# A cached-attention decode kernel: K in whole softmax blocks, query broadcast by PE, one loop per engine

## Chip, cores, metric

One core of one Trainium2 chip. The metric is the device time of one execution in microseconds (us); lower is better. A change counts as faster or slower when it moves the time by more than 2%.

## The reference

One token attends to 65536 cached keys in each of 16 heads; the result is gated by a small MLP and added to the input. Cut to what matters:

```python
B, Sq, D = 1, 1, 448
H, Sk, Dh = 16, 65536, 256            # k_cache, v_cache: 1 x 16 x 65536 x 256, bfloat16
xn = _layernorm(x)
q = (xn @ wq).reshape(B, Sq, H, Dh).transpose(0, 2, 1, 3)
scores = jnp.einsum("bhqd,bhkd->bhqk", q, k_cache) * (Dh ** -0.5)
p = _softmax(scores, axis=-1)
o = jnp.einsum("bhqk,bhkd->bhqd", p, v_cache)
s = o.transpose(0, 2, 1, 3).reshape(B, Sq, H * Dh) @ wo
g = silu(silu(xn @ w1) @ w2)
return x + s * g
```

K and V are 1074 MB together, the weights some 10 MB. Each cached number is used once.

## The kernel before

The cache is cut into 64 blocks of 128 x 128 keys, four for each head. A partition holds 128 keys of a block, 64 KiB. VectorE (DVE) computes 19 of every 32 dot products with a fused multiply-add and multiplies the other 13 in one instruction; ScalarE (ACT) sums those 13. Then comes a softmax over the block with the block's own maximum, and TensorE (PE) multiplies the weights by V. The blocks' results are combined at the end. SP issues all large loads, in order, into one queue. K and V come in tiles of 64 keys per partition (32 KiB), two tiles of each.

```python
KT = 64; SUB = 32; ND = 19; TPB = 2
Kt = [pool.tile([P, KT * Dh], bf16, name=f"K{t}") for t in range(TPB)]
Vt = [pool.tile([P, KT * Dh], bf16, name=f"V{t}") for t in range(TPB)]
...
def take(e, s, k=1):                       # wait for a semaphore and take k from it
    e.wait_ge(s, k).then_inc(s, -k)

def sp_block(i):
    for t in range(TPB):
        take(sp, kf[t])                    # K's tile is free
        sp.dma_start(out=Kt[t][:, :], in_=src(Kd, i, t)).then_inc(kl[t], 16)
        take(sp, vf[t])                    # V's tile is free
        sp.dma_start(out=Vt[t][:, :], in_=src(Vd, i - 1, t)).then_inc(vl[t], 16)

def dve_block(i, first=False, halves=False):
    q_t = own(dve.tensor_copy(out=qcur[:, :], in_=qb[:, sub(q0, Dh)]))
    for t in range(TPB):
        for s in range(2):                 # four steps of 32 keys
            k = t * 2 + s
            if s == 0:
                take(dve, kl[t], 16)       # half a block has landed
            ...
            m = dve.tensor_tensor(out=prod[k % 2][:, :, :], ...)       # 13 keys, for ACT
            if (k == 0 and not first) or (k == 2 and halves):
                dve_gmax()                 # global maximum of the block before
            for j in range(ND):            # 19 keys, fused
                ins = dve.tensor_tensor_reduce(out=junk_d[jk][:, :], ...,
                    accum_out=S[:, k * SUB + j : k * SUB + j + 1])
    ...
    end(0, TPB * KT, kf[1])                # copy S, row maximum for PE

with nc.Fori(1, NBLK - 1, 1, engines={ET.PE, ET.DVE, ET.Activation, ET.SP}, ...) as i:
    sp_block(i)
    dve_block(i)
    act_block(i)
    act_keep(i - 1)
    pe_bcast()                             # global maximum to all partitions
    pe_attend()                            # weights times V
    pe_rows()                              # row maxima to one row
    pe_turn()                              # turn the block's result
...
# after the loop: the last V has a place of its own, W, where the query's weights lay
take(sp, vf[0])
halves(Vt[0], src(Vd, last, 0), vh[0:2])
halves(W, src(Vd, last, 1), vh[2:4])
...
pe_bcast()
pe_attend(between=half_max)                # V's first tile, then half_max
half_max()                                 # pe_rows(), pe_bcast()
```

## Time and profile before

| | before |
|---|---|
| time, median of 4 runs | 2528.03 us (2527.88 to 2528.26) |
| span of the profiled execution | 2527.2 us (that execution took 2529.32 us, 1.3 above the median) |
| mean granted TensorE clock | 0.727 |
| DVE busy | 2219.2 us, 88% |
| DMA, rate from 300 to 2300 us, from the packet records | 431.7 GB/s |

The page, the windows and DVE's steps are shown in the prediction below. Timeline columns: start, duration, engine, line, operation, output<-inputs, count, and in brackets the idle time before it with what ended it.

```profile
2470.90 9.02 PE L308 MATMUL psO<-V,PV 128*2 128x512 bf16 x32 [7.32 <-PEq L141]
...
2486.54 9.73 PE L308 MATMUL psO<-V,PV 128*2 128x512 bf16 x32 [5.24 <-PEq L141]
...
2498.88 8.69 PE L308 MATMUL psO<-V,PV 128*2 128x512 bf16 x32
...
2518.48 4.70 PE L679 MATMUL ps_ao<-K,OT 128*1 128x448 bf16 x24
```

A block's V is 64 matmuls, half of it 32. The last block but one is multiplied at 2470.90 and 2486.54, as its two tiles come. From 2486.54 PE hardly waits again, and ends at 2518.48 + 4.70 = 2523.2. The last byte of data lands about 2517.3.

### The profile page before, as it was taken

To read this page: it belongs to the slowest core of one execution; us is meant where nothing else is said; L and a number is where in the kernel's file an instruction comes from. 1 tells how busy PE (TensorE), PEld (TensorE's weight loads), DVE (VectorE), ACT (ScalarE), POOL (GpSimd) and SP (SyncE) were. 2 spreads that over 40 slices of the span, in tenths; PEclk is the share of its full clock that TensorE was granted. 3 is DMA by queue.
4 is the path that set the end of the run, shared out by engine and by line. 5 is a ranking of instruction groups with operands and counts; after the bars stand their busy time and mean duration, and the time that the engine had idled before them with its cause. 6 is when DMAs were issued, how large, how long until landed. Compare 5 with 4: busy or idle time off the path is not lost. (4 is left out here: it accounts for less than half of the span.)

```text
span 2527.2 us, 30558 instructions
## 1 busy us (share of the span) xinstructions
PE 1284.5 (51%) x4945; PEld 483.4 (19%) x4945; DVE 2219.2 (88%) x10276; ACT 1446.6 (57%) x6996; POOL 1.4 (0%) x12
## 2 busy tenths in 40 slices
PE   3554455455544554555455445544554455445547
PEld 1111121111111211111112111111121111111212
DVE  7989898898898988988989889889898898898886
ACT  5656565655565656555656565556565655565553
POOL 0000000000000000000000000000000000000000
PEclk7777777777777777777767776777677767776778
DMA  9999999999999999999999999999999999999998
GB/s 413 432 432 432 432 432 432 432 432 432 432 432 433 432 433 432 432 432 432 432 432 432 432 432 432 432 432 432 432 432 432 432 432 433 432 432 432 432 432 346
DMA packets 40450, 1084.46 MB, mean 429 GB/s; under 512 B 4338, under 2 KB 6516, under 8 KB 6644
## 3 DMA queue, kind: packets, MB, share of 16 engines
q1 hardware_dynamic: 40434, 1084.31, 99.8%
q8 instruction: 4, 0.07, 0.0%
q14 instruction: 10, 0.08, 0.0%
q10 hardware_dynamic: 2, 0.00, 0.0%
HBM read 1084.29 MB, written 0.00 MB: 429 GB/s over the span
## 5 line engine op out<-in xcount | busy, mean ns | idle before, releaser
L262 ACT ACTIVATE junk_a<-prod 128x256 bf16<-128x256 bf16 x3328 | 1330.7, 401 | 746.9 <-ACTq L141 746.9
L308 PE MATMUL psO<-V,PV 128*2 128x512 bf16 x4064 | 1165.2, 458 | 1097.6 <-PEq L141 1097.6
L226 DVE CUSTOM_DVE_ANT_0 junk_d<-K,qcur 128x256 bf16<-128x256 bf16 x4864 | 1698.7, 414 | 0.0
L308 PEld LDWEIGHTS psO<-V,PV 128*2 128x2 bf16 x4064 | 388.4, 97 | 1847.6 <-issue 1520.3
L212 DVE TENSOR_TENSOR prod<-K,qcur 128x3328 bf16<-128x3328 bf16 x256 | 482.9, 1886 | 247.0 <-DVEq L141 247.0
L262 ACT ACTIVATION_READ_ACCUMULATOR junk_a<-prod 128x1 f32 x3328 | 620.0, 186 | 0.0
L226 DVE DVE_READ_ACCUMULATOR2_ANT S<- 128x1 f32 x4864 | 374.2, 77 | 0.0
L295 ACT COPY O<-psO 2x512 f32<-2x512 f32 x64 | 36.8, 574 | 202.4 <-ACTq L141 202.4
L343 PE MATMUL ps_t<-eye,O 2*128 2x1 f32 x520 | 69.6, 251 | 48.4 <-PEq L141 48.4
L343 PEld LDWEIGHTS ps_t<-eye,O 2*128 2x128 f32 x520 | 65.9, 192 | 69.0 <-issue 68.9
L297 ACT COPY hist<-ps_t 128x2 f32 (+1 forms) x65 | 10.4, 160 | 94.9 <-ACTq L141 94.9
L301 PE MATMUL ps_nb<-gmax,ones_row 1*128 1x1 bf16 x65 | 10.3, 159 | 56.1 <-PEq L141 55.6
L191 DVE COPY qcur<-qb 128x256 bf16 (+1 forms) x64 | 14.5, 227 | 25.4 <-issue 15.8
L284 ACT ACTIVATE PV<-S,hist 128x128 bf16<-128x128 f32 (+1 forms) x65 | 26.0, 400 | 2.1
L199 DVE COPY S<-S 128x128 f32<-128x128 f32 (+1 forms) x65 | 14.7, 226 | 9.5
L200 DVE TENSOR_REDUCE rmax<-S 128x1 bf16<-128x128 f32 (+1 forms) x65 | 18.2, 280 | 0.2 <-issue 0.2
L180 DVE TENSOR_REDUCE gmax<-ps_m 1x1 bf16<-1x128 f32 x65 | 17.8, 274 | 0.5 <-DVEq L141 0.5
L301 PEld LDWEIGHTS ps_nb<-gmax,ones_row 1*128 1x128 bf16 x65 | 6.0, 92 | 60.8 <-issue 60.5
L333 PE MATMUL ps_m<-ident,rmax 128*1 128x128 bf16 x65 | 14.3, 220 | 5.7 <-PEq L141 5.7
L488 PE MATMUL ps_a<-xnT,V 128*64 128x1 bf16 x112 | 6.7, 256 | 18.2 <-DMA V<-in_B_w_dram 18.2
L284 ACT ACTIVATION_READ_ACCUMULATOR PV<-S,hist (+1 forms) x65 | 12.1, 186 | 0.0
L488 PEld LDWEIGHTS ps_a<-xnT,V 128*64 128x64 bf16 x112 | 6.6, 210 | 18.7 <-DMA V<-in_B_w_dram 18.7
(65 smaller groups left out, 79.3 us busy)
## 6 DMA issues: line engine op xcount, KB each, us to landing
K<-in_A_k_cache_dram SPq DMA_DIRECT2D x126, 4096.0 KB, 21.3
V<-in_A_v_cache_dram SPq DMA_DIRECT2D x125, 4096.0 KB, 28.7
K<-in_A_k_cache_dram SPq DMA_DIRECT2D x4, 2048.0 KB, 18.5
V<-in_A_v_cache_dram SPq DMA_DIRECT2D x4, 2048.0 KB, 22.9
W<-in_A_v_cache_dram SPq DMA_DIRECT2D x2, 2048.0 KB, 27.3
W<-in_A_wq_dram SPq DMA_DIRECT2D x1, 3072.0 KB, 10.4
K<-in_A_wo_dram SPq DMA_DIRECT2D x3, 896.0 KB, 31.4
V<-in_B_w_dram SPq DMA_DIRECT2D x1, 1568.0 KB, 35.5
```

The lines of the kernel that those rows point to most:

```text
L180: dve.reduce_max(out=gmax[0:1, :], in_=ps_m[0:1, :], axis=AX.X).then_inc(gm, 1)
L191: q_t = own(dve.tensor_copy(out=qcur[:, :], in_=qb[:, sub(q0, Dh)]))
L199: dve.tensor_copy(out=S2[:, c0:c1], in_=S[:, c0:c1]).then_inc(f, 1)
L200: dve.reduce_max(out=rmax[:, :], in_=S[:, c0:c1], axis=AX.X).then_inc(rm, 1)
L212: m = dve.tensor_tensor(out=prod[k % 2][:, :, :], in0=Kv[:, s * SUB + ND : (s + 1) * SUB, :], in1=qcur[:, None, :].to_broadcast([P, NA, Dh ...
L226: ins = dve.tensor_tensor_reduce(out=junk_d[jk][:, :], in0=Kv[:, s * SUB + j, :], in1=qcur[:, :], scale=1.0, scalar=0.0, op0=ALU.mult, op1 ...
L262: ins = act.activation(out=junk_a[jk][:, :], in_=prod[k % 2][:, j, :], func=ACT.Identity, accum_out=S[:, a : a + 1],)
L284: act.activation(out=PV[:, c0:c1], in_=S2[:, c0:c1], func=ACT.Exp, bias=neg, scale=scale, accum_out=hist[:, at(i), 1:2].rearrange("p o s - ...
L295: act.copy(out=O[:, :], in_=po[:, :]).then_inc(oc, 1)
L301: pe.matmul(ps_nb[:, 0:1], lhsT=ones_row[0:1, :], rhs=gmax[0:1, :], start=True, stop=True).then_inc(bm, 1)
L308: ins = pe.matmul(po[:, :], lhsT=PV[:, c0 + c : c0 + c + 2], rhs=T[:, (k0 + c) * Dh : (k0 + c + 2) * Dh], start=(start and c == 0), stop=( ...
L343: ins = pe.matmul(ps_t[:, a : a + 1], lhsT=Ov[:, j, a, :], rhs=eye2[:, j : j + 1], start=(j == 0), stop=(j == 1),)
```

## The change

The intent is fewer and larger transfers and less bookkeeping: K comes as whole blocks in two slots (64 KiB rows, one DMA for each of 63 blocks in place of two; the last still comes in halves), V stays in halves. To find that room, the products overwrite K and the multiplied tile, the query of all heads is no longer kept on every partition (PE broadcasts the head's query once per block), and `W` goes. Each engine gets its own loop; DVE's has two blocks in its body, with a prefetch hint at the branch. DVE now takes its own block's global maximum before it starts the next. The tail is rewritten. The core, with cuts marked by `...`:

```diff
-KT = 64
+KB = 128
+VT = 64
-    Kt = [pool.tile([P, KT * Dh], bf16, name=f"K{t}") for t in range(TPB)]
-    Vt = [pool.tile([P, KT * Dh], bf16, name=f"V{t}") for t in range(TPB)]
-    W = pool.tile([P, max(DF * HD + HD // 2, NHA * D, KT * Dh)], bf16, name="W")
-    prod = [pool.tile([P, NA, Dh], bf16, name=f"prod{i}") for i in range(2)]
-    qb = pool.tile([P, HD], bf16, name="qb")
+    Kt = [pool.tile([P, KW], bf16, name=f"K{t}") for t in range(2)]
+    Vt = [pool.tile([P, VW], bf16, name=f"V{t}") for t in range(2)]
+    prod = pool.tile([P, NA, Dh], bf16, name="prod")
+    q16 = pool.tile([H, Dh], bf16, name="q16")
 ...
+    def load_k(i, s):
+        take(sp, kf[s])
+        sp.dma_start(out=Kt[s][:, :], in_=block(Kd, i)).then_inc(kl[s], 16)
 ...
+        def end(c0, c1, own):
+            ...
+            dve.tensor_copy(out=S2[:, c0:c1], in_=S[:, c0:c1]).then_inc(kf[s], 1)
+            dve.reduce_max(out=rmax[:, :], in_=S[:, c0:c1], axis=AX.X).then_inc(rm, 1)
+            dve_gmax()
+        take(dve, qr)
+        dve.tensor_copy(out=qcur[:, :], in_=ps_q).then_inc(sd, 1)
+        take(dve, kl[s], 16)
+        for k in range(NSTEP):
 ...
                 ins = dve.tensor_tensor_reduce(
-                    out=junk_d[jk][:, :],
+                    out=Kv[:, c, :],
 ...
+    def pe_block(i):
+        take(pe, pv)
+        for t in range(2):
+            take(pe, vl[t], 16)
+            pe_keys(psO, Vt[t], 0, PV, t * VT, VT, t == 0, t == 1, vf[0] if t == 0 else od)
+        pe_rows()
+        pe_turn(vf[1])
+        pe_bcast()
+        pe_query(i + 1)
 ...
+        with loop(ET.SP, 0, NBLK - 4, 2) as i:
+            for s in range(2):
+                load_v(i + s)
+                load_k(i + s + 2, s)
 ...
+        with loop(ET.DVE, 0, NBLK - 2, 2, hint_back_edge=True) as i:
+            for s in range(2):
+                dve_block(s)
 ...
+        project(0)                         # tail: 8 heads' output projection
+        pe_rows()                          # row maxima of half the last block
+        pe_bcast()
+        take(pe, pv)
+        take(pe, vl[0], 16)
+        pe_keys(psO, Vt[0], 0, PV, 0, VT, True, False, vf[0])
+        ...                                # rest of the last block but one
+        act_keep(LAST - 1)
+        pe_turn()
```

## The prediction

The sum: 2528 + 5 - 2 - 1.5 = 2529.5, and 1.5 more for the fetch rival makes the 2531. The quarter for the fetch, the 1% and both ends of the range are estimates. The query matmul's 0.25 us, inside DVE's 2.5, was estimated as half the mean of 458 ns that the page before gives for a 512-column matmul.

> **What bounds the kernel now.** I read the page first (engines, slices), then the table of windows, the SP queue's waits, and the timeline of DVE and PE at a block's edge and in the tail. The page:
>
> ```profile
> span 2527.2 us, 30558 instructions
> PE 1284.5 (51%) x4945; PEld 483.4 (19%) x4945; DVE 2219.2 (88%) x10276; ACT 1446.6 (57%) x6996; POOL 1.4 (0%) x12
> DMA  9999999999999999999999999999999999999998
> GB/s 413 432 432 432 432 432 432 432 432 432 432 432 433 432 433 432 432 432 432 432 432 432 432 432 432 432 432 432 432 432 432 432 432 433 432 432 432 432 432 346
> HBM read 1084.29 MB, written 0.00 MB: 429 GB/s over the span
> ```
>
> DVE at 88% looks like the limit, but DMA is full in every slice but the first and the last, at a constant 432 GB/s, and 1084.29 MB at 432 GB/s is 2510 us of the 2527. The windows say the same, and where the other 17 us are:
>
> ```profile
> 0.00:2.00 2.00, 0.00 (x0) 0.00 (x0) 0.00 (x0) 0.00 (x0) 1.02 (x10) 1.00 0.00 0
> 60.00:2440.00 2380.00, 1205.84 (x4539) 448.55 (x4540) 2115.26 (x9813) 1376.48 (x6684) 0.00 (x0) 0.72 1.00 432
> 2470.00:2504.00 34.00, 25.85 (x95) 9.57 (x96) 30.76 (x134) 18.24 (x88) 0.00 (x0) 0.78 1.01 428
> 2504.00:2517.00 13.00, 13.00 (x66) 5.69 (x65) 2.30 (x8) 1.52 (x4) 0.00 (x0) 1.00 0.95 360
> ```
>
> (Columns: window, length, busy us of PE, weight loads, DVE, ACT, POOL, then clock, DMA share, GB/s.) Two us pass before the first byte; from 60 to 2440 us the DMA share is 1.00; data end near 2517; the rest is PE's tail (its last projection ends at 2523.2), two DVE steps and the output's transfer. A block is 8.39 MB of K and 8.39 MB of V, so the block's period is 16.78 MB / 432 = 38.8 us, 64 times. DVE is busy about 34.5 of them.
>
> DVE's steps, at the end of a block and in the tail, where the row-maximum chain runs with nothing queued before it:
>
> ```profile
> 1206.56 1.89 DVE L212 TENSOR_TENSOR prod<-K,qcur 128x3328 bf16<-128x3328 bf16 x1
> 1208.37 0.42 DVE L226 CUSTOM_DVE_ANT_0 junk_d<-K,qcur 128x256 bf16<-128x256 bf16 x1
> ...
> 1214.59 0.42 DVE L226 CUSTOM_DVE_ANT_0 junk_d<-K,qcur 128x256 bf16<-128x256 bf16 x1
> 1214.93 0.08 DVE L226 DVE_READ_ACCUMULATOR2_ANT S<- 128x1 f32 x1
> 1215.16 0.23 DVE L199 COPY S<-S 128x128 f32<-128x128 f32 x1
> 1215.31 0.28 DVE L200 TENSOR_REDUCE rmax<-S 128x1 bf16<-128x128 f32 x1
> ```
>
> ```profile
> 2496.18 0.21 DVE L200 TENSOR_REDUCE rmax<-S 128x1 bf16<-128x64 f32 x1
> 2496.54 0.22 PE L333 MATMUL ps_m<-ident,rmax 128*1 128x128 bf16 x1 [0.27 <-PEq L141]
> 2496.91 0.28 DVE L180 TENSOR_REDUCE gmax<-ps_m 1x1 bf16<-1x128 f32 x1 [0.51 <-DVEq L141]
> 2497.33 0.16 PE L301 MATMUL ps_nb<-gmax,ones_row 1*128 1x1 bf16 x1 [0.57 <-PEq L141]
> 2497.48 1.07 PE L343 MATMUL ps_t<-eye,O 2*128 2x1 f32 x8
> ```
>
> A step of one multiply and 19 fused multiply-adds is 1214.93 - 1206.56 = 8.37 us. In the second fence each hop between DVE and PE costs about 0.15 us.
>
> [...] the built program's DVE loop has 171 instructions, and between 94 and 2478 us the packet records hold no instruction fetch. The new DVE loop has 339[...].
>
> **The change part by part.**
>
> Bytes: none removed or added. The kernel stays at 2510 us of transfer unless the rate changes.
>
> K in 64 KiB rows. The packet records give a median of 613 ns for 16 KiB and 1218 for 32 KiB: 605 for the second 16 KiB, so about 8 ns are fixed. If a 64 KiB row is one packet, each saves 8 ns: 8 packets per engine and block, 64 blocks, 4.1 us. If it is cut into 32 KiB again, 0. I take 2.
>
> DVE per block, where K is already there: four steps 4 x 8.37 = 33.5 (destination and semaphores change, operand sizes do not). Last fused step to end of row maximum: 1214.93 to 1215.59, 0.66. Then the chain that was hidden in the next block is now on DVE's path, as DVE takes its own global maximum before the next block, and the query comes from PE after PE's turn of the output: hop 0.15, rows 0.22, turn 1.07, global-max broadcast 0.16, query matmul about 0.25 [...], hops 0.3, then the query copy from PSUM, about 0.4 (estimates from the 128-column copy, 0.23). Together about 2.5. DVE's cycle is 33.5 + 0.66 + 2.5 = 36.7 us, longer than before but 2.1 below the DMA's 38.8. ACT's 13 sums take 5.3 us from 0.2 after the multiply, done 1.1 us before the step's end, so one product buffer instead of two costs nothing.
>
> PE per block: two halves of 9.1 to 9.6 us and the small ones, about 21 of 38.8. Not the bound.
>
> Does DMA still always have work? The second half of a block's V waits for PE's turn, which now comes after the end of DVE's next block; so does the K load two blocks on. In steady state DVE's end lies 38.8 - 34.2 = 4.6 us before the next K lands, and half a block of V (9.7 us) is queued behind that K. Some 14 us of work are queued when the issue comes: no gap.
>
> Start: this is where I see a loss. The queue is weights (6.9 MB), K0, K1, V0: K0 lands whole at about 38 us (before, DVE could start on half of it near 21), K1 at 57, V0 at 77. DVE ends block 0 at 38 + 34.5 = 72.5 and block 1 at 72.5 + 36.7 = 109. The queue behind V0 is K2 (to 96) and half of V1 (to 106). The other half of V1 and K3 are released by the end of block 1: first bytes near 111. DMA is idle some 5 us, once. After that DVE gains 2.1 us per block and the margin grows. Against about 0.6 us of loss in before's 40 to 60 us window: +5.
>
> Tail: eight of 16 heads' projection (16 of 32 matmuls of about 0.2 us, 3 us) move ahead of the last V; the last V comes in smaller pieces. In exchange the last DVE block ends 16 us before the last byte instead of 21, still early enough. PE's tail from the last byte: before 2523.2 - 2517 = 6; I get about 5. -1 to -2.
>
> Preamble (64 query matmuls of 16 rows, the diagonal copies): hidden under K0's landing at 38.
>
> Sum: 2528 + 5 (start) - 2 (packets) - 1.5 (tail) = 2529.5. I put 2531 for the rival below.
>
> **The rivals.**
>
> (1) Instruction fetch. [...] But the fetches take time on a DMA engine, and a transfer is done only when its slowest engine is. The trace's 8 KiB instruction packets took 309 ns[...]. [...] I give it a quarter. If the branch also stalls for longer than the two blocks' slack of 4.2 us, DVE becomes the bound: 5 us over it is 31 x 5 = 155, 2680; 5%.
>
> (2) DVE as the bound through the turn-around: each us above 38.8 in its cycle costs 63 us. My 36.7 would have to be 5.7% low. The four steps are measured, so the error must be in the 2.5 us; 4.6 would be needed. Against it: the tail's hops are short. 4%.
>
> (3) The transfer gets faster: [...]
>
> (4) Hidden anyway: everything off DMA's path, 2527 to 2529.
>
> **Range and chances.** Most of the weight lies at 2520 to 2535; the fetch rival stretches the upper side. Centre 2531, range 2517 to 2560. Faster by over 2% would need under 2478[...]: 1%. Slower by over 2% is over 2579: only a bound moved to DVE or a bad fetch: 6%. Within 2%: 93%.
>
> **What would show it.** Right: DMA share 1.00 and 432 to 434 GB/s from 150 us on; a dip in DMA between about 105 and 112 us; DVE busy still near 34.5 of 38.8 us per block, with its idle in two places, some 2 us before the query copy (new) and some 2 before the first multiply (K landing). The packet counts say whether 64 KiB rows are one packet or two. Wrong: a DMA share below 1.00 in the middle, with SP waiting for K's or V's release; DVE with no wait for K; instruction packets in every round; idle DVE at the loop's branch every second block; fused steps slower than 0.346 us apart because they write into K.

## The result and the profile after

| | before | after |
|---|---|---|
| time, median of 4 | 2528.03 us | 2538.82 us (2538.12 to 2539.02) |
| ratio after/before | | 1.0042, 95% interval 1.0025 to 1.0059 |
| span of the profiled execution | 2527.2 us | 2536.9 us |
| clock | 0.727 | 0.713 |

A ratio here is the mean time of one kernel's fast runs over that of the other's fast runs of the same rounds, so not quite the ratio of the medians quoted. The verdict is the same within 2%; the predicted 2531 was 8 us low, inside its range. The profiled executions differ by 9.35 us in time and 9.7 in span; the medians differ by 10.8, because before's profiled execution was 1.3 us above its median. I account for the 9.7.

The page of the kernel after, the lines that answer to those of before:

```profile
span 2536.9 us, 30448 instructions
PE 1217.3 (48%) x5050; PEld 505.8 (20%) x5050; DVE 2234.0 (88%) x10281; ACT 1443.7 (57%) x6991; POOL 2.5 (0%) x13
DMA  9899999999999999999999999999999999999997
GB/s 413 381 432 438 426 433 431 434 433 438 427 433 431 435 441 422 435 432 430 435 441 422 438 430 430 441 427 430 438 430 430 442 426 438 430 430 433 434 419 310
```

The kernel is still bound by DMA; what is lost shows at the edges: 381 in the second slice where before had 432, and 419 and 310 at the end against 432 and 346. The unevenness between (422 to 442) I take for counting, as packets are now up to 64 KiB; the ledger below has an even slope.

**The ledger.** To see where time goes in a kernel bound by transfers, I laid the two packet records over each other: the time at which so many MB had come, from each kernel's first packet, with a packet's bytes spread evenly over its duration. Figures are us; from the third column on, lateness against before.

| MB come | before | after | K in halves | turn last | early start 2 | combined 3 |
|---|---|---|---|---|---|---|
| 40 | 94.3 | +0.2 | 0.0 | 0.0 | -0.4 | -0.4 |
| 50 | 117.4 | +7.8 | +7.6 | +6.6 | +1.1 | +0.2 |
| 100 | 233.2 | +7.4 | +7.6 | +6.2 | +0.8 | 0.0 |
| 400 | 928.1 | +6.0 | +7.5 | +4.8 | -0.6 | -1.4 |
| 1000 | 2317.8 | +3.1 | +7.4 | +1.8 | -3.5 | -4.3 |
| 1060 | 2456.7 | +2.9 | +7.5 | +1.7 | -3.6 | -4.4 |
| 1065 | 2468.4 | +3.9 | +8.3 | +2.6 | 0.0 | -1.9 |
| 1084.2 (end) | 2515.3 | +3.9 | +7.7 | +2.1 | -0.9 | -2.0 |

The column "after" reads: one hole between 40 and 50 MB costs 7.8 us; a slightly higher rate then wins 4.9 of it back over the whole cache; the tail costs 1.0. Data end 3.9 us later than before. The last matmul ends at 2532.9 against 2523.2, 9.7 later, so PE's tail behind the last byte has grown by 9.7 - 3.9 = 5.8 us (from 5.9 to 11.7). 7.8 - 4.9 + 1.0 + 5.8 = 9.7, the span's whole difference. The other columns belong to experiments below.

**The hole.** Before's windows from 104 to 112 us, then after's from 104 to 116 and from the middle (window, length, busy us of PE, weight loads, DVE, ACT, POOL, clock, DMA share, GB/s):

```profile
104.00:108.00 4.00, 4.00 (x16) 1.37 (x14) 3.33 (x20) 2.17 (x12) 0.00 (x0) 0.74 1.05 451
108.00:112.00 4.00, 2.05 (x10) 0.62 (x8) 2.15 (x2) 0.13 (x1) 0.00 (x0) 1.00 0.91 393
```

```profile
104.00:108.00 4.00, 0.00 (x0) 0.00 (x0) 4.00 (x20) 3.10 (x15) 0.00 (x0) 0.50 0.63 270
108.00:112.00 4.00, 0.00 (x0) 0.00 (x0) 3.78 (x22) 2.66 (x13) 0.00 (x0) 0.50 0.02 8
112.00:116.00 4.00, 2.62 (x12) 2.02 (x13) 1.71 (x3) 0.82 (x4) 0.00 (x0) 0.50 0.55 180
...
1000.00:2000.00 1000.00, 479.57 (x1939) 195.40 (x1939) 898.39 (x4148) 582.73 (x2830) 0.00 (x0) 0.71 1.00 433
```

By the shares, after's DMA is empty from about 106.5 to 114. SP has nothing that it may load: the second half of the next V and the next K wait for buffers that come free only with the end of DVE's second block and the turn behind it; SP issues the two at 113.08 and 113.67. In the middle the share is 1.00 again, and stays there.

**DVE's edge of a block.** The timeline of the first one, where nothing waits for DMA:

```profile
74.41 0.28 DVE L223 TENSOR_REDUCE rmax<-S 128x1 bf16<-128x128 f32 x1
...
74.84 0.27 PE L318 MATMUL bank<-ident,rmax 128*1 128x128 bf16 x1 [39.22 <-PEq L153]
...
75.03 1.86 PE L334 MATMUL bank<-eye,O 2*128 2x1 f32 x8
75.25 0.28 DVE L212 TENSOR_REDUCE gmax<-bank 1x1 bf16<-1x128 f32 x1 [0.56 <-DVEq L153]
...
76.76 0.16 PE L324 MATMUL bank<-gmax,ones_row 1*128 1x1 bf16 x1
...
76.79 0.37 PE L348 MATMUL bank<-q,ident 16*128 16x256 bf16 x1
...
77.31 0.43 DVE L227 CAST qcur<-bank 128x256 bf16<-128x256 f32 x1 [1.77 <-DVEq L153]
77.77 1.89 DVE L235 TENSOR_TENSOR prod<-K,qcur 128x3328 bf16<-128x3328 bf16 x1
```

From the end of the row maximum (74.69) to the next multiply (77.77) is 3.08 us, in which DVE works 0.71 and waits 0.56 and 1.77, the two waits in brackets. The longest link is the turn, L334, 1.86 us (eight small matmuls by which PE brings a block's output from two rows back onto the partitions): PE had been idle for 39 us and ran at half clock. In the prediction's row the same eight matmuls took 1.07, behind 9.73 us of matmuls on V. The trace's clock is 0.50 until 82.5 us here, 4.0 us after PE began on V at 78.46, and 1.00 from 2492.0 to 2498.8 around the prediction's row. In the middle of the kernel after it is the same as here: the turn at 1226.16 takes 1.86 us, at a clock of 0.50.

**The tail.** DVE of the kernel after: one line of the last block but one, and the row maxima of the last block's two halves:

```profile
2445.75 0.08 DVE L246 DVE_READ_ACCUMULATOR2_ANT S<- 128x1 f32 x1 [2.50 <-issue]
...
2492.52 0.22 DVE L223 TENSOR_REDUCE rmax<-S 128x1 bf16<-128x64 f32 x1
2493.30 0.28 DVE L212 TENSOR_REDUCE gmax<-bank 1x1 bf16<-1x128 f32 x1 [0.56 <-DVEq L153]
...
2510.57 0.22 DVE L223 TENSOR_REDUCE rmax<-S 128x1 bf16<-128x64 f32 x1
```

and PE:

```profile
2478.87 4.74 PE L631 MATMUL bank<-K,OT 128*1 128x448 bf16 x16 [6.35 <-DMA K<-in_A_wo_dram]
2492.89 0.27 PE L318 MATMUL bank<-ident,rmax 128*1 128x128 bf16 x1 [9.27 <-PEq L153]
...
2494.03 16.47 PE L306 MATMUL bank<-V,PV 128*2 128x512 bf16 x64
2511.34 1.07 PE L334 MATMUL bank<-eye,O 2*128 2x1 f32 x8 [0.84 <-PEq L153]
...
2531.19 1.67 PE L631 MATMUL bank<-K,OT 128*1 128x448 bf16 x8
```

Before took the two maxima at 2478.75 and 2496.18; after takes them at 2492.52 and 2510.57, 14 us later. PE stands idle for 9.27 us until 2492.89, because its queue has the row maxima of the last block's first half ahead of the V of the block before. Only then do the 64 matmuls of that V begin, of which before had done 32 by 2480.

### The profile page after: what moved, and what is told of

Its sections match the earlier page's. It is cut to its first block, busy times and chain, and to the rows that moved or that the text cites. A ratio compares the mean times of both kernels' runs of the same rounds, so it can differ in the third digit from the quotient of the medians.

```text
span 2536.9 us, 30448 instructions
## 1 busy us (share of the span) xinstructions
PE 1217.3 (48%) x5050; PEld 505.8 (20%) x5050; DVE 2234.0 (88%) x10281; ACT 1443.7 (57%) x6991; POOL 2.5 (0%) x13
## 2 busy tenths in 40 slices
DMA packets 31221, 1084.48 MB, mean 427 GB/s; under 512 B 3298, under 2 KB 5476, under 8 KB 5604
## 3 DMA queue, kind: packets, MB, share of 16 engines
q1 hardware_dynamic: 31202, 1084.31, 99.2%
## 5 line engine op out<-in xcount | busy, mean ns | idle before, releaser
L267 ACT ACTIVATE prod<-prod 128x256 bf16<-128x256 bf16 x3328 | 1330.7, 401 | 792.7 <-ACTq L153 792.7
L246 DVE CUSTOM_DVE_ANT_0 K<-K,qcur 128x256 bf16<-128x256 bf16 x4864 | 1702.3, 428 | 0.0
L306 PE MATMUL bank<-V,PV 128*2 128x512 bf16 x4064 | 1029.8, 418 | 718.3 <-PEq L153 717.8
L306 PEld LDWEIGHTS bank<-V,PV 128*2 128x2 bf16 x4064 | 360.6, 90 | 1372.9 <-issue 956.9
L267 ACT ACTIVATION_READ_ACCUMULATOR prod<-prod 128x1 f32 x3328 | 619.9, 186 | 0.0
L246 DVE DVE_READ_ACCUMULATOR2_ANT S<- 128x1 f32 x4864 | 440.0, 90 | 2.5 <-issue 2.5
L227 DVE CAST qcur<-bank 128x256 bf16<-128x256 f32 x64 | 27.2, 425 | 117.3 <-DVEq L153 117.3
L334 PE MATMUL bank<-eye,O 2*128 2x1 f32 x528 | 120.6, 345 | 0.8 <-PEq L153 0.8
L334 PEld LDWEIGHTS bank<-eye,O 2*128 2x128 f32 x528 | 115.0, 315 | 11.3 <-issue 2.1
L293 ACT COPY O<-bank 2x512 f32<-2x512 f32 x66 | 36.9, 559 | 4.8 <-ACTq L153 4.8
```

What stands on the lines that cost most here:

```text
L227: dve.tensor_copy(out=qcur[:, :], in_=ps_q).then_inc(sd, 1)
L246: ins = dve.tensor_tensor_reduce(out=Kv[:, c, :], in0=Kv[:, c, :], in1=qcur[:, :], scale=1.0, scalar=0.0, op0=ALU.mult, op1=ALU.add, accum ...
L267: ins = act.activation(out=prod[:, j, :], in_=prod[:, j, :], func=ACT.Identity, accum_out=S[:, c : c + 1],)
L293: act.copy(out=O[:, :], in_=po).then_inc(oc, 1)
L306: ins = pe.matmul(po, lhsT=W[:, c0 + c : c0 + c + 2], rhs=T[:, (k0 + c) * Dh : (k0 + c + 2) * Dh], start=(start and c == 0), stop=(stop an ...
L334: ins = pe.matmul(ps_t[:, a : a + 1], lhsT=Ov[:, j, a, :], rhs=eye2[:, j : j + 1], start=(j == 0), stop=(j == 1),)
```

## The experiments

All eleven runs gave correct results. Intervals of the ratios are about 0.0017 wide each way, 4 us, so for most of these the traces carry the verdict and the times only agree with it. The kernel after has ratio 1.0042 to compare with. Runs 1, 2, 4 and 5 were made on one chip, where before took 2529.5 us, the others on another, where it took 2528.0 and single executions of it spread from 2527.7 to 2531.0. So medians of different runs are not to be subtracted, and a difference of 1 or 2 us between two single traces (runs 5 and 6) is no larger than that spread.

**Theories.** A: three terms, each with its place: a hole at the start because DVE gets K late and frees it late; one packet in place of two for each 64 KiB row; a tail in which PE waits for DVE. B, the rival from the prediction: DVE's loop of 339 instructions is fetched anew or stalls. C: the edge of a block on DVE's path costs in every block.

**1. K in halves.** K comes as two 32 KiB DMAs on the same semaphore, the first two blocks (not shown in the cut) too; all else stays.

```diff
-        sp.dma_start(out=Kt[s][:, :], in_=block(Kd, i)).then_inc(kl[s], 16)
+        for z in range(2):
+            sp.dma_start(out=Kt[s][:, z * VW : (z + 1) * VW],
+                in_=block(Kd, i)[:, z * VW : (z + 1) * VW]).then_inc(kl[s], 16)
 ...
-        take(dve, kl[s], 16)
+        take(dve, kl[s], 16 if halves else 32)
```

> Every whole K load is cut in two of 32 KiB per partition on the same semaphore; all else as in the changed kernel. Theory (rows of 64 KiB move faster): the middle falls from 432.7 to 431.7 GB/s as in the kernel before, so about 5 to 6 us are lost over 1084 MB: 2544 us (2543 to 2546). Rival (the rate has another cause, such as the order of the loads): stays at 2538 to 2540. No packet of 64 KiB is left in either case.

Measured: 2542.77, ratio 1.0054, span 2540.9, just under the expected range. The packets between 300 and 2300 us, for before, after and this kernel:

```profile
DMA packets 29645, 863.42 MB, mean 432 GB/s; under 512 B 3296, under 2 KB 3296, under 8 KB 3296
```

```profile
DMA packets 22330, 865.41 MB, mean 433 GB/s; under 512 B 2480, under 2 KB 2480, under 8 KB 2480
```

```profile
DMA packets 29636, 863.58 MB, mean 432 GB/s; under 512 B 3282, under 2 KB 3282, under 8 KB 3282
```

A 64 KiB row is one packet: the kernel after has 8064 packets of 65536 bytes, median 2421 ns, this one none. Two packets of 32 KiB take 2 x 1217 = 2434. In the ledger the lateness stays at 7.4 to 7.6 us here where after's falls from 7.8 to 2.9. The ten other runs, which load all or nearly all of K whole, fall by 4.1 to 4.9 between the same marks, 50 and 1060 MB. The term is shown, at 4 to 5 us. The edit also doubles K's DMAs and with them the 4-byte records that each DMA leaves (4306 against 3298, 9 ns each, some 0.6 us for each engine); the run does not separate these from the size of the rows.

**2. Early start.** The MLP's weights are loaded first, then the query's, then the first K in halves; DVE's first two blocks come ahead of its loop. PE's code for the MLP moves ahead of its code for the query (not shown in the cut).

```diff
-        load_rows(wq_t, A_wq, HD, dl["wq"])
         load_rows(w12_t, B_w1, F, dl["w12"])
         sp.dma_start(out=w12_t[:, w2_at:w12_w], ...).then_inc(dl["w12"], 16)
-        for s in range(2):
-            sp.dma_start(out=Kt[s][:, :], in_=block(Kd, s)).then_inc(kl[s], 16)
+        load_rows(wq_t, A_wq, HD, dl["wq"])
+        load_keys(Kt[0], 0, block(Kd, 0), 0, VT, kl[0])
+        load_keys(Kt[0], 0, block(Kd, 0), VT, KB, kh)
+        sp.dma_start(out=Kt[1][:, :], in_=block(Kd, 1)).then_inc(kl[1], 16)
 ...
+        dve_block(0, first=True)           # takes kh before its third step
+        dve_block(1)
-        with loop(ET.DVE, 0, NBLK - 2, 2, hint_back_edge=True) as i:
+        with loop(ET.DVE, 2, NBLK - 2, 2, hint_back_edge=True) as i:
```

> The MLP's weights are loaded and used first, then the query's, and the first K block comes in two halves with DVE's first two blocks outside the loop, so that DVE starts near 29 us in place of 40. Theory (the one gap of some 8 us in the transfers near 107 to 115 us is DVE running late after the wait for the whole first K block): the gap goes, 7 to 8 us less: 2531 us (2530 to 2533). Rival (the gap comes from PE's release of V, or DVE isn't what is late): the gap stays and so does 2539, or less than 3 us are won.

Measured: 2534.95, ratio 1.0021, span 2534.0. A partial hit: the hole shrank from 7.8 to 3.4 us. PE did the MLP's second product before the query, and ACT, which had the query at 32.64, began its first sums late:

```profile
38.66 0.42 ACT L269 ACTIVATE prod<-prod 128x256 bf16<-128x256 bf16 x1 [6.02 <-ACTq L153]
```

Those 6.02 us are not a wait for DVE, whose first product was ready some 3 us earlier: in the trace ACT's sequencer takes the branch into its loop at 32.35, runs its next instruction at 38.49 and comes to the wait for DVE at 38.57. What ACT stood still for is not shown: one 8 KiB instruction packet lies in that time, at 36.82, but no run isolates it.

**3. Early start 2.** The same, with the query ahead of the MLP's second product.

```diff
         t = silu(h1s[:, :], ps_h, h1e[:, :], t)
+        need("pe", t7)
+        pe.wait_ge(dl["wq"], 32)
+        ...                                # query of all heads, first broadcast
         w2_v = w12_t[:, w2_at:w12_w].rearrange("p (f d) -> p f d", d=D)
```

> As early_start, but PE makes the query before the MLP's second product: in early_start the query was ready only at 32.7 us and ACT's first sums began 3 us late [...], so DVE's block 0 ended at 70.3 in place of 74.7. Theory (the gap is as long as DVE is late): the query is ready near 27.5 us, the first half of K0 lands near 29, block 0 ends near 64, block 1 near 101, before the queue runs dry near 106: gap 0 to 1 us, 7 to 8 us less than the changed kernel, 2531 to 2532 and about 3.5 under early_start. Rival (something else holds V or K back): the gap of early_start, 3.4 us, stays.

Measured: 2534.45, ratio 1.0025, span 2532.1: in the transfers a hit, in the time a miss by some 3 us. The hole is gone (1.1 us in the ledger), and at 1060 MB this kernel is 3.6 us ahead of before. But by 1065 MB it is level: the queue ran dry there, as the tail's first loads wait for the end of DVE's block 62. Of 6.7 us won at the start, 4.8 reached the span. The start term is shown; part of it was covering a wait in the tail.

**4. Tail, rows later.** If PE wastes 9.27 us on the row maxima, let it multiply V first.

```diff
         project(0)
-        pe_rows()
-        pe_bcast()
         take(pe, pv)
         take(pe, vl[0], 16)
         pe_keys(psO, Vt[0], 0, PV, 0, VT, True, False, vf[0])
+        pe_rows()
+        pe_bcast()
```

> In the tail PE no longer waits for the half maximum of the last block before it starts on the first half of the last V but one: row maximum and broadcast come after those 32 matmuls. Theory (the tail is longer because PE sat idle for 9 us, from 2484 to 2493, and then has 39 us of work in a row): PE starts at about 2488, when that V lands, 5 to 6 us less: 2533 us (2532 to 2535). Rival (the tail is set by the last bytes): 0 to 1 us less, 2538.

Measured: 2543.71, ratio 1.0057, span 2541.8: a miss, slower. DVE's and PE's timelines say why:

```profile
2497.26 0.28 DVE L212 TENSOR_REDUCE gmax<-bank 1x1 bf16<-1x128 f32 x1 [4.74 <-DVEq L153]
```

```profile
2488.30 8.75 PE L306 MATMUL bank<-V,PV 128*2 128x512 bf16 x32 [5.10 <-PEq L153]
...
2513.73 1.83 PE L334 MATMUL bank<-eye,O 2*128 2x1 f32 x8 [8.83 <-PEq L153]
```

PE now starts at 2488.30, when V lands, 5.7 us sooner. But DVE takes its maximum between the halves of its own block, so it waits 4.74 us for PE; its end slips by 4.0 us, from 2510.8 to 2514.7; ACT, which keeps the result only after its last sums, slips with it; and PE waits 8.83 us for ACT. The two queues wait on each other in a cross: whichever comes first, the other pays.

**5. No hint.** Against rival B.

```diff
-        with loop(ET.DVE, 0, NBLK - 2, 2, hint_back_edge=True) as i:
+        with loop(ET.DVE, 0, NBLK - 2, 2) as i:
```

> The branch prefetch hint [...] is left out. Theory [...]: no instruction packets in the loop, time unchanged at 2539. Rival (the loop is kept from fetching by the hint): without it, two or more instruction packets of 8 KiB every 77.6 us, DVE idle of 1 us or more at the branch every second block; DVE has only about 3 us of slack per two blocks (cycle 37.2 of 38.8), so a stall of 3 us costs nothing and one of 6 us costs 31 x 3 = 90 us: 2540 to 2640.

Measured: 2536.69, ratio 1.0029, span 2535.3. The kernel after has no instruction packet between 83 and 2443 us of its span, this one a single one of 8 KiB at 99.2 us and none from there to 2445, so the loop of 339 instructions (338 without the hint) is not fetched again in its rounds, hint or not. What came with the hint is the 2.50 us of "issue" in the DVE lines shown above. They lie in block 62, the first block behind the loop, and an 8 KiB instruction packet lies in them, from 2443.85 to 2444.18. All nine kernels with the hint have such a stall in block 62, of 2.24 to 2.84 us; the three changed kernels without it have none, and here the four steps of block 62 come 8.37 us apart. B is refuted, and its sign too: the hint cost 2.5 us on DVE. The span is 1.6 shorter, in a run whose transfers were 1.1 us behind after's at 1060 MB.

**6. Turn last.** Against C: PE does rows, query and broadcast before the turn, which takes the slow 1.86 us out of DVE's path.

```diff
         pe_rows()
-        pe_turn(vf[1])
-        pe_bcast()
         pe_query(i + 1)
+        pe_bcast()
+        pe_turn(vf[1])
```

> In PE's loop the query and the global-max broadcast come before the turn of the output, so that DVE waits less between blocks: from 3.1 us (row maximum's end to next multiply) to about 1.3. Theory (DVE has slack of 1.5 us per block in the middle, so its turn-around counts only while DVE runs late, in the first two blocks): the gap near 107 to 115 us shrinks by 1 to 2 us, the middle stays at the DMA's rate; 1 to 2 us less than the changed kernel, 2537 to 2538. Rival (the turn-around is on the path in each block): 1.8 us x 62 = over 100 us less; not possible beyond the DMA's rate, so it would show as a rise above 433 GB/s in the middle.

Measured: 2537.53, ratio 1.0037, span 2535.3. The ledger is 1.2 us lower at 50 MB and keeps just that distance to after all the way (7.8 - 6.6, 2.9 - 1.7). So the edge of a block is paid once, at the start, and not in the blocks behind: in the kernel after DVE works off its delay by the tenth block (377 us), and from there waits 1.6 us for K in each. C is refuted.

**7. Tail reordered.** V's first half of the last block but one is queued ahead of the first piece of `wo` and used first; the whole first half of the last V ahead of the second row maximum; ACT keeps the result between its third and fourth sums.

```diff
+        take(sp, vf[0])
+        load_keys(Vt[0], 0, Vn, 0, VT, vl[0])
         take(sp, kf[0])
         ...                                # wo, first piece
-        take(sp, vf[0])
-        load_keys(Vt[0], 0, Vn, 0, VT, vl[0])
 ...
         act_sums(2)
+        act_keep(LAST - 1)
         act_sums(3)
```

> Tail: the first half of V of the last block but one is queued before the first part of the output weights and used by PE before it; both quarters of the last V that lie in K's slot are used before the second half maximum; ACT moves the output of the last block but one before its last sums. Row maxima are still served at once, which tail_rows_later did not do. Theory (in the tail DVE and ACT wait for PE and PE for ACT, because each serves its own order; tail_rows_later only moved the wait to DVE, which then ended the last block 4 us later): DVE ends the last block at 2510 as before, PE has then only the last V half and the projection left: last matmul near 2525 in place of 2533, 6 to 8 us less, 2531 to 2533. Rival (DVE's end alone sets the tail): under 2 us less.

Measured: 2536.62, ratio 1.0032, span 2535.0: 1.9 us won, less than expected. V landed 4.1 us sooner than in run 4 (PE starts at 2484.18), but 32 matmuls of 9.74 us together (the next 32 took 7.07) and the projection's 3.19 came before the row maxima, and DVE waited again:

```profile
2497.16 0.28 DVE L212 TENSOR_REDUCE gmax<-bank 1x1 bf16<-1x128 f32 x1 [4.21 <-DVEq L153]
```

**8. Combined.** Early start 2, turn last, tail reordered and no hint together.

> early_start2, turn_last and tail_reordered together, without the prefetch hint (which was seen to stay without use in the loop and to go with a stall of 2.5 us after it). Theory: the gains add, -7.5 (start), -7 (tail), -2 (hint), turn_last nothing more as the gap is gone: 2522 us (2520 to 2524), some 6 us under the kernel before. Rival (the tail's gain and the start's gain overlap or DMA ends set both): 2525 to 2529.

Measured: 2533.30, ratio 1.0019, span 2531.7: a miss. DMA led before by 4.1 us at 1060 MB, but DVE waited 4.55 us for its half maximum and the last matmul ended at 2527.7. The gains at the start do not pass through a tail that PE sets.

**9. Tail in two banks.** Takes the cross apart: V's matmuls are cut at 8, 16 and 32 with rows and broadcast between, and the last block goes to a second PSUM bank, so that the turn no longer stands between.

```diff
-        pe_rows()
-        pe_bcast()
         take(pe, pv)
         take(pe, vl[0], 16)
-        pe_keys(psO, Vt[0], 0, PV, 0, VT, True, False, vf[0])
+        pe_keys(psO, Vt[0], 0, PV, 0, VT // 4, True, False)
+        pe_rows()
+        pe_keys(psO, Vt[0], VT // 4, PV, VT // 4, VT // 4, False, False)
+        pe_bcast()
+        pe_keys(psO, Vt[0], VT // 2, PV, VT // 2, VT // 2, False, False, vf[0])
 ...
-        pe_keys(psO, vlast, 0, PV2, 0, VT // 2, True, False)
+        pe_keys(psO2, vlast, 0, PV2, 0, VT // 2, True, False)
 ...
         pe_rows()
+        pe_turn()
         pe_bcast()
```

> Tail: PE starts on V of the last block but one as soon as it lands and serves the half maximum in between, after eight of its matmuls; the last V's first half goes to another PSUM bank, so it need not wait for ACT's move of the block before, which comes after ACT's last sums. The order of loads is that of the changed kernel. tail_reordered won only 2 us: PE's first V landed at 2484, then 13 us of PE work stood before the half maximum and DVE waited 4.2 us for it. Theory (the tail is PE's work from the landing of that V on, 2488, lengthened by crossed waits): DVE waits under 1.5 us for either half maximum, PE has no wait over 2 us after 2489, last matmul near 2527 in place of 2533: 5 to 6 us less than the changed kernel, 2533 us (2532 to 2535). Rival (DVE's end of the last block, 2510.5, plus 22 us of work behind it): 0 to 2 us less, 2537 to 2539.

Measured: 2534.94, ratio 1.0029, span 2532.8, with the last matmul at 2528.8 in place of 2532.9. PE:

```profile
2488.20 3.56 PE L306 MATMUL bank<-V,PV 128*2 128x512 bf16 x8 [5.13 <-PEq L153]
2492.54 0.22 PE L318 MATMUL bank<-ident,rmax 128*1 128x128 bf16 x1 [0.78 <-PEq L153]
2492.59 1.89 PE L306 MATMUL bank<-V,PV 128*2 128x512 bf16 x8
...
2494.51 10.52 PE L306 MATMUL bank<-V,PV 128*2 128x512 bf16 x48
```

After 2488 no wait of PE is longer than 1.1 us, and DVE's wait for the half maximum is 0.51. The 4.1 us are 1.0 in the transfers (2.8 us behind before at 1060 MB and still 2.8 at the end, where after went from 2.9 to 3.9) and 3.1 on PE. The cross is shown, at 4.1 of the 6.8 us that the tail had lost; the edit moves pieces, turn and bank together, so the 4.1 belong to all of them.

**10. Weights later.** DVE's weights of the first 15 heads move behind the last block, to start that block sooner, and with them the projection of 8 heads. One round only.

```diff
         dve_block(0)
         tt = pe_sums(ps_tot[:, 0:N1], 0, N1)
-        weights(0, N1, 0, H1, (ps_tot[:, 0:N1], tt))
-        t_o = outputs(0, N1, 0, H1)
-        dve_block(1, halves=True)
+        ...
+        dve_block(1, halves=True, between=first_heads)   # the two calls above
```

> DVE's eleven small steps for the first 15 heads' weights come after the last block's steps in place of before them, and the projection of the first eight heads moves behind. Theory (PE's work from the landing of V at 2488 on sets the tail): DVE ends its last block 4.5 us earlier, at 2506, but PE has the same work left and 3 us of projection more: 0 to 2 us won, 2537 to 2539. Rival (DVE's end sets the tail): 4 to 5 us won, 2534.

Measured: 2541.82 (2 runs), ratio 1.0053, span 2540.4: a miss in sign. DVE's last block started only 2 us sooner, since the query then had to be waited for, and the second row maximum came at 2508.56 in place of 2510.57, but PE lost more:

```profile
2490.88 0.27 PE L320 MATMUL bank<-ident,rmax 128*1 128x128 bf16 x1 [17.45 <-PEq L153]
...
2520.61 3.19 PE L636 MATMUL bank<-K,OT 128*1 128x448 bf16 x16
```

The projection's 3.19 us had lain in PE's idle time and now lies behind V, and 16 of the matmuls before it took 5.30 us in place of 3.61. DVE came 2 us sooner and the last matmul 3.5 us later: here what PE still has to do sets the finish, and not DVE's end.

**11. Combined 3.** Early start 2, turn last, the tail in two banks, no hint; five rounds.

> early_start2, turn_last, tail_two_banks, and no prefetch hint. Theory: start -7.3 us as measured by the transfers of combined (they led those of the kernel before by 4 us at 1050 MB, where the changed kernel's lagged by 2.9), tail -5.5, hint's stall -2.5 where DVE counts: last matmul near 2521, 2525 to 2527 us, so 1 to 3 us under the kernel before. Rival (the tail stays as in combined, 2533): 2530 or more.

Measured: 2531.18 (2530.74 to 2532.68, 6 runs), before in the same rounds 2528.05; ratio 1.0011, interval 0.9998 to 1.0025. Again above what was expected. Data end 2.0 us ahead of before, but PE has too much left:

```profile
2484.71 3.57 PE L308 MATMUL bank<-V,PV 128*2 128x512 bf16 x8 [4.08 <-PEq L153]
...
2491.13 10.52 PE L308 MATMUL bank<-V,PV 128*2 128x512 bf16 x48
2501.49 7.31 PE L308 MATMUL bank<-K,PV 128*2 128x512 bf16 x32
...
2525.19 1.67 PE L638 MATMUL bank<-K,OT 128*1 128x448 bf16 x8
```

From 2484.71 to 2526.9 is 42 us, with only 2.6 us of marked waits; before needed 36.6 from 2486.54, having done 32 of these matmuls earlier. This recovers most of the loss (ratio 1.0042 to 1.0011) but no version beats before. Of its 4.4 us of lead at 1060 MB, 2.5 are lost by 1065 MB, in the wait for block 62 as in run 3. I did not try the version that also queues V ahead of `wo` there: I expect that even with the wait gone, PE's work would have held the end close to where before has it; this is not shown.

## Why the prediction was right

Right, for the reason given: the bytes are the same and DMA stays the bound, so a rearrangement of everything else moved only the edges. That the time fell into the range owes something to luck: 2538.82 lies above the 2520 to 2535 that had most of the weight, in the part kept for the fetch rival, which did not come. The prediction's terms add up to +1.5, the measured ones to +9.7, and the tail makes most of the difference. Point by point:

- **DVE in place over K costs nothing: right.** Steps are still 8.37 us apart.
- **DVE's cycle stays under DMA's: right, with a mis-sized term.** The turn-around was put at 2.5 us and measured 3.08, because the turn's 1.07 came from a row at a clock of 1.00 and the loop's turn runs at 0.50 (1.86). From one first multiply to the next is 115.00 - 77.77 = 37.23 us in place of 36.7. The slack of 1.6 us per block still covers it; run 6 shows that nothing of it reaches the middle.
- **No instruction fetch in the loop, which the prediction left at three chances in four: right.** Run 5 shows it (no instruction packet between 83 and 2443 us with the hint, one at 99.2 without), and shows that the hint did no good. (The prediction's 94 and 2478 us count from the first packet record, 11 us before the span; on the span's clock they are 83 and 2467. Its clause on the slowest engine holds in the trace: V's half issued at 113.08 left 16 end records between 124.20 and 124.74, and landed at 125.11, after the last.)
- **The start hole, +5: right place, too small.** It measured 7.8. K landed at 40.40 and DVE's first multiply came at 40.53 and not 38, and the turn-around was longer. (Before had started at 18.1, on a quarter of the block, and not near 21 on half of it.) Runs 3 and 6 move it as the mechanism says.
- **Packets, -2: right in sign, too small.** The doubt was whether a row is one packet. It is (8064 packets of 65536 bytes), and the gain is 4.9, above the full 4.1 too, with 432.7 GB/s between 300 and 2300 us in place of 431.7; run 1 takes it away again.
- **The tail, -1.5: this step failed.** It measured +6.8: 1.0 in the transfers, 5.8 on PE. "The last DVE block ends 16 us before the last byte instead of 21, still early enough" was wrong twice. It ended 10.5 before, since the 2.5 us of stall behind the loop and DVE's weights, which stretch the step to the last block from 3.08 to 5.99 us, lie ahead of that block, and I had counted neither. And it was not early enough: I had looked at the end of DVE's block, but PE's queue waits for its middle, and the V of the block before stands behind that wait. Runs 4, 7 and 9 show the cross, run 10 that PE's remaining work and not DVE's end sets the finish.

The errors in start and tail had one sign, the packets the other; that the total was within 8 us owes something to that. What stays open: the last 2.7 us of the tail (6.8 less the 4.1 of run 9), which I put down to 32 matmuls being done later than before without having measured it alone, and what ACT stood still for in run 2.

## What to carry to other kernels

When a kernel is bound by bytes, lay the cumulative bytes of both traces over each other before explaining anything: holes, slopes and ends separate at once, and each can be tested alone. Larger tiles made transfers cheaper by a little here (2421 ns for 64 KiB in place of 2 x 1217), but what waited for a whole tile started later and freed it later, which was paid once at the start (a hole of 7.8 us) and once at the end (some of the tail's 6.8). Where two in-order queues waited for each other in turn, moving one wait only handed it to the other (runs 4 and 7: DVE waited 4.74 and 4.21 us in place of 0.56); cut the long run of work into pieces around it (run 9: 0.51), and take durations for small matmuls from a place with the same clock (the turn: 1.86 us at 0.50, 1.07 at 1.00).
